# The second batch's q by bf16 split and crossbar transposes, and an earlier load of w_tok's last rows, in a fused attention and mixer kernel

## The chip, the cores and the metric

The kernel runs on one core of one Trainium2 chip. The metric is the device time of one execution in microseconds (us), lower is better. Each run carries its mean granted TensorE clock (1.0 is full speed) and a state: a run over 1.5% above the fastest of its kernel is called slow. Engines are called PE (TensorE), PEld (its weight loads), DVE (VectorE), ACT (ScalarE), POOL (GpSimd) and SP (SyncE, which issues nearly all DMAs here). In the profile, L549 is line 549 of the kernel.

## The reference, cut to what matters

```python
kv  = einsum('bhsd,bhse->bhde', k, v)          # batch 8, heads 8, seq 576, head_dim 64
out = einsum('bhsd,bhde->bhse', q, kv)
x   = out / sqrt(mean(out*out, -1) + 1e-6) * g_norm     # then heads are put side by side: d_model 512
a1  = alpha1 * x + beta1
tok = einsum('ts,bsd->btd', w_tok, a1)          # token mixing, 576 x 576
u   = x + lam * tok
a2  = alpha2 * u + beta2
ch  = maximum(a2 @ w_ch1, 0) @ w_ch2            # channel MLP, 512 -> 2048 -> 512
return u + lam * ch                             # all float32
```

## The kernel before

The eight batches run in a software pipeline: while PE works on the channel MLP of batch b, the attention and token mixing of batch b+1 and the k-by-v products of batch b+2 are slipped in between. A scheduler inside the kernel's own code decides, when the kernel is built, in which order each engine runs its instructions. It goes by costs written into the code (`P.op(engine, cost_us, ...)`). On the chip every engine then runs its list in that order. `at=` gives an operation a fixed rank, `slack` lets it be placed later. A wrong cost doesn't break anything, but it can leave the order a poor one.

Tile names met below: kf, vf and qf hold k, v and q as loaded; qs and qst the bf16 halves of q, qt and qtt the same transposed (qst and qtt for the tail rows); kvd the bf16 form of kv; sq and small the squares and sums of the normalisation, xm the rows of x and later of u, rt the bf16 input of the token mixing, wst and wt w_tok as loaded and transposed; a2b and a2t the MLP's input, ht its hidden values; stg the three staging buffers of the weights; ps is PSUM.

q must be transposed before the products q times kv. The first two batches (`R32 = 2`) do that on PE in fp32. From the third batch on, q is split into a high and a low bf16 half (ACT casts, DVE or POOL subtracts), and six DMA transposes through the crossbar, issued by SP, do the transposing:

```python
R32 = 2
...
def split_q(b):                       # five pieces: ACT makes hi, DVE or POOL makes lo = q - hi
    for x in range(5):
        ...
        P.op("ACT", act_us(n), lambda e, ...: copy(e, hi, src), r=kin, w=[("qs", x, 0)])
        P.op(dve_pool(n), 0, lambda e, ...: e.tensor_tensor(out=lo, in0=src, in1=hi, op=ALU.subtract), ...)

def qt_dma(b):                        # six transposes: four into qt, two for the tail into qtt
    for a in range(3):
        for y in range(2):
            ...
            P.op("SP", 1.3, lambda e, o=o, i_=i_: e.dma_start_transpose(o, i_), ...,
                 w=[("qt", a, y)], dma_us=0.8 if a < 2 else 0.3, slack=SLACK)
```

The loads leave SP in a fixed order. w0 to w3 are the 1 MB slices of W_ch1, w4 to w7 those of W_ch2, Bk, Bv and Bq the second batch's k, v and q, t0 to t2 rows of w_tok:

```python
order = ["k0", "v0", "q0", "k1", "t0", "v1", "q1", "t1",
         "w0", "g", "w1", "w2", "Bk", "Bv", "w3", "Bq", "lam", "a2", "t2", "w4",
         "w5", "w6", "w7"]
```

Each slice of W_ch2 is multiplied by lam on its way into bf16, on DVE or POOL, whichever the scheduler picks.

```python
for hh in range(4):
    P.op(dve_pool(512), 0, lambda e, hh=hh: e.tensor_tensor(              # L1270
        out=w2[:, 4 * n + hh, :], in0=stg[:, i % 3, hh], in1=lam_bc[:], op=ALU.mult), ...)
```

Of the kernel before, what the change touches and what calls it, by code (L numbers as in the profile page):

```python
# [403 lines left out]
def bass_transnormer_attn__then__resmlp_affine_kernel(  # L404
# [15 lines left out]
    with ExitStack() as stack:  # L420
        P = Prog(nc, stack)
# [27 lines left out]
        qtt = sb("qtt", [128, NH, 128], BF16)  # L449
# [47 lines left out]
        ALL = (slice(0, 8),)  # L497
        R32 = 2
        SLACK = 5.0
# [20 lines left out]
        def split_q(b):  # L520

            for x in range(5):
                if x < 4:
                    src = qf[:, x, 0:8].rearrange("p (k r) d -> p r k d", r=2)
                    hi, lo = (qs[:, x, :, i, :].rearrange("p (r k) d -> p r k d", r=2)
                              for i in range(2))
                else:
                    src = qf[:, :, 8, :]
                    hi, lo = (qst[:, :, i, :] for i in range(2))
                n = 512 if x < 4 else 256  # L530
                kin = [("qf", x // 2)] if x < 4 else [("qf", 0), ("qf", 1)]
                P.op("ACT", act_us(n), lambda e, hi=hi, src=src: copy(e, hi, src),
                     r=kin, w=[("qs", x, 0)])
                P.op(dve_pool(n), 0, lambda e, hi=hi, lo=lo, src=src: e.tensor_tensor(  # L534
                    out=lo, in0=src, in1=hi, op=ALU.subtract), r=kin + [("qs", x, 0)],
                    w=[("qs", x, 1)], port=True)

        def qt_dma(b):
            lo = 64 * (b % 2)
            for a in range(3):  # L540
                for y in range(2):
# [4 lines left out]
                    else:  # L546
# [4 lines left out]
                            for i in range(2)],  # L551
                         w=[("qt", a, y)], dma_us=0.8 if a < 2 else 0.3, slack=SLACK)

# [109 lines left out]
        def qkv_groups(b):  # L663

            def group(cs, hs):
# [20 lines left out]
                def f32(e):  # L686
                    if nc_ > 1:
                        for h in range(nh):
                            w = qtr[:, h0 + h, 2 * cs[0]:2 * cs[0] + 2, :].rearrange(
                                "p k s -> p (k s)")  # L690
                            for x in range(1 if nh < 8 else 2):
                                y = slice(0, 128) if nh < 8 else slice(64 * x, 64 * x + 64)
                                o = (t.flat().rearrange("p (c h d) -> p c h d", c=2, d=64)[
                                    :, :, h, :] if nh < 8 else t.cols(64 * (nh * x + h), 64))
                                mm = e.matmul(o, w, kvr[:, h0 + h, y], start=True, stop=True)  # L695
                    else:
                        for h in range(h0, hs.stop):
                            p = 64 * (h // 4)
                            mm = e.matmul(t.flat()[:, 64 * (h - h0):64 * (h - h0) + 64],
                                          qtrt[:, h % 4, :], kvr[:, h, p:p + 64],  # L700
                                          start=True, stop=True)
                    return mm
                if b < R32:
                    P.op("PE", 0.058 * m, f32, cold=True,
                         r=["qtp", "kvz"] + [("qtr", a, cs[0] if nc_ > 1 else 2) for a in aa] + [
# [42 lines left out]
                else:  # L748
# [14 lines left out]
                    out=x3, in0=x3, in1=gb, op=ALU.mult), r=xk + ["g"], w=xk, pri=-50, port=True)  # L763
            for hs in (HALVES if b == 0 else ALL):
                for cs in ((0, 2), (1, 3), (4,)):
                    yield lambda cs=cs, hs=hs: group(cs, hs)
# [313 lines left out]
        def params_late():  # L1080
            for key in ("e1r", "lamr", "gr", "er", "ebh", "ebl", ("pc", 0), ("pc", 1)):
                for n in range(4):
# [4 lines left out]
        order = ["k0", "v0", "q0", "k1", "t0", "v1", "q1", "t1",  # L1087
                 "w0", "g", "w1", "w2", "Bk", "Bv", "w3", "Bq", "lam", "a2", "t2", "w4",
                 "w5", "w6", "w7"]
# [7 lines left out]
        for x in range(2):  # L1097
            for u in (2 * x, 2 * x + 1):
# [3 lines left out]
        P.op("SP", 0.6, lambda e: e.dma_start(wst4[:], moe_w_tok[8:576:9, :]),  # L1102
             w=[("wst", 4)], dma_us=0.9, at=sp["t2"])
        for n, dst, src in (("lam", lam_bc, moe_lam), ("a2", a2_bc[:], moe_alpha2),
# [119 lines left out]
        def run(gens):  # L1224
            for gen in gens:
                for f in gen:
                    f()
# [59 lines left out]
        u0 = P.lastw[("a2t", 0)] + P.lastw[("a2t", 2)]  # L1287
        run([kv_groups(1), qt_groups(1)])
        for i in range(4, 8):
# [16 lines left out]
        for b in range(NB):  # L1306
# [5 lines left out]
            merge(ch1, list(qkv_groups(b + 1)), 0, len(ch1) * 5 // 8)  # L1312
            if b == 0:
                last = [o for a in range(2) for m in range(3) for o in P.readers[("qtr", a, m)]]
                for key in ([("qt", a, y) for a in range(3) for y in range(2)] +
                            [("qs", x, i) for x in range(5) for i in range(2)]):
                    P.readers.setdefault(key, []).extend(last)
            if more:
# [5 lines left out]
            if more:  # L1324
                if b == 0:
                    P.op("POOL", 0.9, lambda e: e.memset(qtt[:], 0.0),
                         w=[("qt", 2, y) for y in range(2)])
                split_q(b + 2)
                qt_dma(b + 2)
# [43 lines left out]
```

## Time and profile before

| | before |
|---|---|
| median of 3 runs (range) | 365.87 us (364.91 to 366.12) |
| span of the profiled run, clock | 364.2 us, 0.993 |
| PE busy | 357.3 us, 98% |
| longest PE wait on a DMA | 1.1 us, for w_tok's last rows |
| first MLP matmul of the second batch (L938) | 82.65 us |

SP's row says when a DMA is issued and how long the issue holds SP. Its columns are start, time, engine queue, line, operation, tiles, count. First the second half of the load phase, then, from the steady part of the kernel, the third batch's six transposes.

```profile
31.76 15.34 SPq L1265 DMA_DIRECT2D stg<-in_moe_w_ch_dram  x4
47.15 0.50 SPq L506 DMA_DIRECT2D kf<-in_k_dram  x1
...
79.67 7.24 SPq L549 DMA_TRANSPOSE qt<-qs  x4
86.95 3.19 SPq L549 DMA_TRANSPOSE qtt<-qst  x2
```

All four slices of W_ch2 are issued by 47.1. The third batch's transposes hold SP for 7.24 + 3.19 = 10.4 us.

### The profile page before, as it was taken

The page shows a single profiled execution, that of the slowest core. Times are in us where ns is not written, and L with a number is a line of the kernel's source. Part 1 is how long each engine was busy: PE and PEld are TensorE (multiplying, and loading weights), DVE is VectorE, ACT ScalarE, POOL GpSimd, SP SyncE. Part 2 cuts the span into 40 slices and gives each one's busy share as a digit, 9 for nine tenths or more (in the row PEclk, how much of TensorE's full clock was granted, in tenths as well). Part 3 has the DMA queues.
Part 4 walks back from the last instruction along what each step waited for, and adds up shares of the span by engine and source line. Part 5 has one row for each costly group of instructions (what it writes and reads, how often), then busy time and mean ns, then how long its engine had stood idle before and what let it go on. Part 6 is the DMA issues. An engine that isn't in the chain of part 4 may idle for free.

```text
span 364.2 us, 8018 instructions
## 1 busy us (share of the span) xinstructions
PE 357.3 (98%) x3594; PEld 215.2 (59%) x3354; DVE 211.4 (58%) x310; ACT 143.7 (39%) x252; POOL 116.2 (32%) x93
## 2 busy tenths in 40 slices
PE   8999899999999999999999999999999999999995
PEld 6888685466754554457654554457754554457644
DVE  3557699872686189823885189724884288620021
ACT  2675057127750158107730157007730156007500
POOL 4377185910064005700281015800751005300000
PEclk9999899999999999999999999999999999999999
DMA  7999996028865677667816684586836510340023
GB/s 286 355 384 363 323 350 250 0 49 113 237 249 117 115 202 283 104 125 170 314 32 127 117 277 174 108 123 142 337 66 124 117 29 2 72 96 21 2 58 86
DMA packets 67558, 59.17 MB, mean 162 GB/s; under 512 B 45552, under 2 KB 45828, under 8 KB 67524
## 3 DMA queue, kind: packets, MB, share of 16 engines
q1 hardware_dynamic: 67472, 58.66, 58.4%
q8 instruction: 27, 0.44, 0.5%
q14 instruction: 7, 0.06, 0.0%
q10 hardware_dynamic: 52, 0.01, 0.0%
HBM read 38.60 MB, written 9.44 MB: 132 GB/s over the span
## 4 chain that ended last, share of the span: by engine, by line
PE 91%; DMA 5%; SPq 2%; ACT 1%; issue 0%; DVE 0%
PE ps L988 34%; PE ps L938 19%; PE ps L923 13%; PE ps L787 8%; PE ps L602 5%; DMA wst<-in_moe_w_tok_dram 3%; DMA vf<-in_v_dram 3%; PE ps L397 2%; PE ps L682 2%; PE ps L1146 2%; PE ps L800 1%; PE ps L695 1%; PE ps L570 1%; SPq L506 1%; PE ps L1189 0%; SPq L1106 0%
## 5 line engine op out<-in xcount | busy, mean ns | idle before, releaser
L988 PE MATMUL ps<-w,ht 128*128 128x512 bf16 (+1 forms) x592 | 129.0, 373 | 0.0
L988 PEld LDWEIGHTS ps<-w,ht 128*128 128x128 bf16 x592 | 56.8, 98 | 64.1 <-issue 1.6
L912 ACT ACTIVATE ht<-ps,bias 128x640 bf16<-128x640 f32 (+2 forms) x98 | 72.5, 742 | 46.4 <-PE ps L938 38.7
L938 PE MATMUL ps<-a2t,w 128*128 128x320 bf16 x512 | 71.9, 299 | 0.0
L762 POOL TENSOR_TENSOR xm<-xm,g_bc 128x1024 f32<-128x1024 f32 (+1 forms) x16 | 33.4, 2085 | 114.9 <-DVE rt L759 112.4
L938 PEld LDWEIGHTS ps<-a2t,w 128*128 128x128 bf16 x512 | 49.5, 98 | 20.3 <-DVE xm L755 0.3
L923 PE MATMUL ps<-a2t,w 128*128 128x512 bf16 x240 | 54.6, 379 | 0.0
L999 DVE TENSOR_TENSOR xm<-ps,xm 128x512 f32<-128x512 f32 (+1 forms) x33 | 22.1, 673 | 53.4 <-PE ps L988 53.4
L633 ACT ACTIVATE kvd<-ps 64x256 bf16<-64x256 f32 x24 | 9.1, 378 | 99.8 <-PE ps L602 99.6
L733 DVE TENSOR_REDUCE small<-sq 128x16 f32<-128x1024 f32 (+3 forms) x27 | 24.8, 928 | 22.9 <-ACT sq L731 22.7
L923 PEld LDWEIGHTS ps<-a2t,w 128*128 128x128 bf16 x240 | 22.7, 98 | 25.1
L787 PE MATMUL ps<-rt,wt 128*128 128x512 bf16 x140 | 31.4, 379 | 0.0
L913 DVE TENSOR_SCALAR ht<-ps,bias 128x512 bf16<-128x512 f32 (+2 forms) x34 | 24.8, 738 | 10.3 <-PE ps L923 4.7
L534 POOL TENSOR_TENSOR qs<-qf,qs 128x512 bf16<-128x512 f32 x14 | 18.5, 1319 | 25.8 <-ACT qs L493 24.8
L731 ACT ACTIVATE sq<-ps 128x1024 f32<-128x1024 f32 (+3 forms) x27 | 21.3, 799 | 12.9 <-PE ps L397 8.2
L771 DVE TENSOR_TENSOR xm<-ps,xm 128x512 f32<-128x512 f32 x28 | 19.1, 688 | 8.9 <-PE ps L787 8.6
L787 PEld LDWEIGHTS ps<-rt,wt 128*128 128x128 bf16 x140 | 13.7, 98 | 16.5
L999 DVE TENSOR_TENSOR xtl<-ps,xtl 128x512 f32<-128x512 f32 x4 | 2.8, 692 | 35.5 <-PE ps L988 35.5
L602 PEld LDWEIGHTS ps<-vf,kf 64*64 64x64 f32 x1152 | 18.9, 140 | 3.5 <-issue 2.5
L602 PE MATMUL ps<-vf,kf 64*64 64x64 f32 x1152 | 20.1, 227 | 0.4 <-DMA vf<-in_v_dram 0.2
L755 DVE TENSOR_TENSOR xm<-ps,small 128x1024 f32<-128x1024 f32 (+1 forms) x18 | 19.7, 1100 | 0.2
L759 POOL TENSOR_TENSOR rt<-xm,e_bc 128x512 bf16<-128x512 f32 (+1 forms) x6 | 9.8, 1635 | 28.4 <-DVE xm L755 27.4
(105 smaller groups left out, 349.5 us busy)
## 6 DMA issues: line engine op xcount, KB each, us to landing
stg<-in_moe_w_ch_dram SPq DMA_DIRECT2D x8, 1024.0 KB, 12.5
kf<-in_k_dram SPq DMA_DIRECT2D x7, 1152.0 KB, 6.6
vf<-in_v_dram SPq DMA_DIRECT2D x7, 1152.0 KB, 8.7
qf<-in_q_dram SPq DMA_DIRECT2D x7, 1152.0 KB, 10.2
out_dram<-xm SPq DMA_DIRECT2D x62, 128.0 KB, 2.4
kf<-in_k_dram SPq DMA_DIRECT2D x2, 576.0 KB, 5.7
vf<-in_v_dram SPq DMA_DIRECT2D x2, 576.0 KB, 9.4
qf<-in_q_dram SPq DMA_DIRECT2D x2, 576.0 KB, 8.3
```

The costliest lines, as they stand in the source:

```text
L602: m = e.matmul(t.ap(slice(64 * i, 64 * i + 64))[:, y, 64 * x_:64 * x_ + 64], kf[rows, x, c], vf[rows, x, c], start=(c == 0), stop=(c == 8) ...
L731: P.op("ACT", act_us(64 * m), lambda e: e.activation(both(sqv), raw(), ACT.Square), r=[t], w=[("sq", sqs)])
L733: P.op("DVE", dve_us(64 * m), lambda e: e.tensor_reduce(out=smv, in_=sqv, axis=AX.X, op=ALU.add), r=[("sq", sqs)], w=[("sm", sms)], pri=-20)
L755: P.op("DVE", dve_us(64 * m), lambda e: e.tensor_tensor(out=x3, in0=raw(), in1=inv(), op=ALU.mult), r=[t, ("sm", sms)], w=xk, pri=-200)
L762: P.op(dve_pool(64 * m) if b < 2 else "POOL", pool_us(64 * m), lambda e: e.tensor_tensor(out=x3, in0=x3, in1=gb, op=ALU.mult), r=xk + ["g" ...
L787: m = e.matmul(t.flat(), wt[:, sc if sc < 4 else 4 + b % 2, 128 * c:128 * c + 128], rt[:, rs(b, sc), :], start=(sc == 0), stop=(sc == 4))
L912: return e.activation(dst, src(), ACT.Relu, bias=bi)
L913: return e.tensor_scalar(out=dst, in0=src(), scalar1=bi, scalar2=0.0, op0=ALU.add, op1=ALU.max)
L923: m = e.matmul(t.flat(), w1[:, dj, 128 * fj:128 * fj + 128], a2t[:, dj, 0:512], start=(dj == 0), stop=(dj == 3))
L938: m = e.matmul(t.ap()[:, i, 0:320], w1[:, dj, 128 * fj:128 * fj + 128], a2t[:, dj, 320 * i:320 * i + 320], start=(dj == 0), stop=(dj == 3))
L988: m = e.matmul(t.flat()[:, 0:m_], ht[:, fj, 128 * c:128 * c + 128], w2[:, fj, lo:hi], start=(fj == 0), stop=(fj == 15))
L999: P.op("DVE", dve_us(m_), lambda e: e.tensor_tensor(out=x, in0=t.flat()[:, 0:m_], in1=x, op=ALU.add), r=[t] + keys, w=keys)
```

## The change

The intent: take the second batch's fp32 transposes and products off PE, which is the bound, by treating that batch like the later ones. To make room, the splits get a rank ahead of W_ch1's last casts, the six transposes get a place ("x") in the load order ahead of W_ch2's last three slices, and w_tok's last rows (t2) go ahead of W_ch1's fourth slice. The scheduler's cost of the remaining fp32 products was corrected too.

```diff
-        R32 = 2
+        R32 = 1
...
                 P.op("ACT", act_us(n), lambda e, hi=hi, src=src: copy(e, hi, src),
-                     r=kin, w=[("qs", x, 0)])
+                     r=kin, w=[("qs", x, 0)], at=-958.5 if b == 1 else None)
... (the same rank for the five subtractions)
-                         w=[("qt", a, y)], dma_us=0.8 if a < 2 else 0.3, slack=SLACK)
+                         w=[("qt", a, y)], dma_us=0.8 if a < 2 else 0.3,
+                         at=sp["x"] + 0.01 * (2 * a + y) if b == 1 else None,
+                         slack=SLACK if b > 1 else 1.0)
...
-                    P.op("PE", 0.058 * m, f32, cold=True,
+                    P.op("PE", 0.1 + (0.06 if nc_ > 1 else 0.12) * m, f32, cold=True,
...
-                 "w0", "g", "w1", "w2", "Bk", "Bv", "w3", "Bq", "lam", "a2", "t2", "w4",
+                 "w0", "g", "w1", "Bq", "w2", "t2", "w3", "lam", "w4", "Bk", "Bv", "x", "a2",
                  "w5", "w6", "w7"]
...
-             w=[("wst", 4)], dma_us=0.9, at=sp["t2"])
+             w=[("wst", 4)], slack=4.0, dma_us=0.9, at=sp["t2"])
...
-        run([kv_groups(1), qt_groups(1)])
+        run([kv_groups(1)])
+        P.op("POOL", 0.9, lambda e: e.memset(qtt[:], 0.0), w=[("qt", 2, y) for y in range(2)])
+        split_q(1)
+        qt_dma(1)
         for i in range(4, 8):
             load_w(i)
... (cut: the fp32 path's code for two batches, and moved bookkeeping)
```

## The prediction

> **What bounds the kernel now.** I read the page first, its engine totals, then its clock row. PE (TensorE) counts as busy for 98% of the span, and the chain that ended last is 91% PE.
>
> ```profile
> PE 357.3 (98%) x3594; PEld 215.2 (59%) x3354; DVE 211.4 (58%) x310; ACT 143.7 (39%) x252; POOL 116.2 (32%) x93
> ...
> PE 91%; DMA 5%; SPq 2%; ACT 1%; issue 0%; DVE 0%
> ```
>
> The reader is to see that no other engine comes near PE, so PE work taken away should come off the end, as long as nothing new stops PE. Next I read the chain of waits in order of time (start, length, what) around the part that the change rewrites, the second batch's attention, at 31 to 55 us.
>
> ```profile
> 31.09 10.16 DMA wst<-in_moe_w_tok_dram
> 41.25 0.14 issue
> 41.38 1.24 PE ps L1146 x16
> ...
> 42.82 3.13 PE ps L602 x138
> ...
> 46.31 1.02 PE ps L570 x8
> 47.34 0.22 PE ps L563 x2
> 47.56 0.86 PE ps L923 x4
> 48.42 0.87 PE ps L570 x8
> 49.29 0.22 PE ps L563 x2
> 49.51 0.86 PE ps L923 x4
> 50.38 3.49 PE ps L695 x32
> 53.87 0.88 PE ps L923 x4
> 54.75 0.81 PE ps L699 x8
> 55.56 4.33 PE ps L923 x20
> ...
> 79.58 2.26 PE ps L602 x144
> ```
>
> L570 and L563 are the fp32 transposes of q, L695 and L699 the fp32 products of q with kv, L602 the k-by-v products, L923 and L988 the channel MLP that fills the time between. The one DMA in this stretch that PE waits for is the transfer of w_tok's last rows (wst): issued at 31.09, landed 10.2 us later. Then I cut PE's row into half microseconds (length, PE busy and instructions, granted clock, DMA share, GB/s).
>
> ```profile
> 40.50:41.00 0.50, 0.00 (x0) 1.00 0.94 283
> 41.00:41.50 0.50, 0.12 (x2) 1.00 1.05 389
> ...
> 42.50:43.00 0.50, 0.50 (x24) 0.50 1.01 373
> ...
> 44.50:45.00 0.50, 0.50 (x30) 0.52 1.05 389
> 45.00:45.50 0.50, 0.50 (x44) 1.00 1.05 389
> ```
>
> This view shows what the busy share hides. PE stands still from 40.24 to 41.38 (1.14 us), and just behind that the granted clock is 0.5 from about 41.5 to 45.0. That is the only half-clock stretch of the run; the 4 us slices from 80 us on are all at 1.00 until the last matmuls.
>
> **What the Trainium skill says.** (1) "TensorE: Matmul & The Clock Gate", Part 1: the array's clock drops to half when a monitoring window of about 3.4 us sees too little PE activity, and comes back after a busy one. The trace agrees on the length (3.5 us at 0.5) but not on the cause as put there, idleness of a whole window: here 1.14 us of idle, beside 0.94 us of two-column bias matmuls, were enough. (2) The same page, LDWEIGHTS: load time follows the weight's columns, not its contraction rows. So cutting the first batch's tail products from 128 to 64 rows (one part of the diff) should give nothing; the trace has no 64-row twin to show it. (3) "DMA: Bandwidth & Descriptors", Rules for kernel authors: a DMA transpose must not run beside one from another queue, but next to ordinary DMAs it needs nothing. All transposes here leave from SP, so none has to be held for that; the trace's batches 3 to 8 already run them so.
>
> **The change, part by part.**
>
> *Removed from PE.* Both transpose groups of the second batch: 46.31 to 47.56 is 1.25 us, 48.42 to 49.51 is 1.09. The products: 50.38 to 53.87 is 3.49, 54.75 to 55.56 is 0.81. Sum 6.64 us, all on the chain.
>
> *Added to PE.* The bf16 form of the same products, as the third batch has them: in its chain they take 92.59 to 94.46 (1.87 us, 64 matmuls) and 96.63 to 97.10 (0.47 us, 16), together 2.34 us. Net 6.64 - 2.34 = **4.30 us off PE**. The k-by-v products stay fp32.
>
> *The w_tok rows ahead of W_ch1's fourth slice.* Before, their issue stood behind that slice's, which waited until 28.32 for a staging buffer, and behind q, lam and alpha2. Now they stand behind slice 3 only, which waits for no buffer; q of the second batch, ahead of it, can go once the first batch's q is transposed (L563 runs at 16.1). By 30 us the DMA of before had moved some 10 MB at about 344 GB/s; in the new order everything up to these rows is 9.1 MB, so about 27 us (an estimate from that rate). PE gets there at 40. So the **1.14 us** gap goes.
>
> *The half clock behind it.* In it the L602 group makes some 61 matmuls per us (30 or 31 per half microsecond), against 98 in the group at 79.58. From 42.7 to 45.0 that is 141 matmuls in 2.3 us in place of 1.4: 0.9 us. The transposes of the w_tok rows before it (1.3 us) would at the same ratio lose another 0.4 to 0.5. If the gap was what tipped the window, **1.3 us** more go. Sum of all gains: 4.30 + 1.14 + 1.3 = 6.7 us.
>
> *Added beside PE.* Five ACT casts for the high halves (the third batch: 4 of 0.615 and 1 of 0.40: 2.9 us), five subtractions (0.68 on DVE or 1.23 on POOL for the large ones: 3.2 to 5.8 us), a 0.95 us memset on POOL that only moves, and six crossbar transposes. From 33 to 46.3 us ACT is busy 2.9 of 13.3 us, POOL 3.7, DVE 9.4: there is room. Evacuations of fp32 q and kv (10 groups on ACT and DVE) become the bf16 pairs for kv. The six transposes take SP from 79.67 to 90.14 in the third batch, 10.5 us. If the splits are done at about 36, their issue ends near 47, the last landing near 49 (2.4 to 4.5 us from issue to landing).
>
> *Moved.* k and v of the second batch now go after W_ch2's first slice. With a DMA at 350 to 390 GB/s from 28 us on (two slices of 1.05 MB, k and v of 1.18 MB each, some 0.3 MB of lam) they land near 43 to 44, by estimate. Before, their products ran at 42.7. W_ch2's slices 2 to 4 now leave behind the transposes, so from about 47, and land near 51 to 58; their first use is about four groups into the L988 run, now near 57.
>
> *What holds the end.* PE work between 39.3 and the second batch's MLP (82.4 before) becomes 43.1 - 6.7 = 36.4 us, so that it would start at 75.7. The dependent path is: transposes landed and kv split at about 49 to 50, new products to about 53, normalisation (55.4 to 63.8 before, but other PE work filled that; DVE's last rt is done at 62.7, so 7.3 us), token mixing 61 to 66.5, then the alpha2 products and transposes (69.7 to 77.9 before: 8 us), so ready near 75. The two paths end within a microsecond of each other. I therefore take **0.8 us** off the gain for stalls: 6.7 - 0.8 = 5.9, and 365.87 - 5.9 = 360.0.
>
> **Rivals.** (a) *The crossbar route comes late.* SP works in a fixed order, splits, then 10.5 us of transposes, then the rest of W_ch2; queued data is 20 MB up to 60 us with the DMA over 0.84 busy nearly all along. If q lands late or the splits slip by 3 us, the new products, token mixing or W_ch2's slice stop PE for 2 to 4 us, and a stop could bring the half clock again. Against: about 20 us of independent MLP work lies there as a filler. This would make 362 to 364. (b) *The splits push W_ch1's casts.* They rank ahead of the last eight casts and of the evacuations of PSUM; late slices 3 and 4 would stop PE near 40 us, 1 to 2 us and perhaps the half clock: 361.5 to 363. For: slice 4 lands only at about 33 to 34. Against: ACT runs nothing from 37 to 42.7 in the profile of before. (c) *More than counted.* The corrected costs of fp32 products may give the scheduler a better start (PE runs warm-up fillers at 26 and 31 us), and the early w_tok rows may fill such holes: up to 1.9 us for their transposes and sums, 358 to 359. Against: their stated slack of 4 us should hold them until after the start. (d) *The clock stays low.* If small matmuls, not the gap, tip the window, 1.3 us remain: 361.3.
>
> **Range and chances.** The clean sum gives 359.2, so 2% (under 358.55) needs all terms and some of (c): 0.15. Rivals (a), (b) and (d) have about one chance in three together and lead to 361.3 to 364. Slower by 2% would need 13 us of new stalls on top of the gain: 0.01. I say 360.0, with 357.8 to 362.9 at 8 in 10.
>
> **What would show it.** Right: no fp32 group of L695's 64-column form any more; 40 more pairs of bf16 products taking 2.3 us; no PE wait on wst; clock 1.00 from 39 to 46; L602's second group at about 2.3 us; the second batch's MLP starting at 75 to 77. Wrong: a PE wait of over 1 us between 36 and 76 us on the transposes, on stg casts or on kf and vf; a new half-clock stretch; or a start (first MLP matmul at 32.2 us) that has moved by more than 1 us either way.

## The result and the profile after

The changed kernel took **375.64 us** (median of 4 runs, 373.78 to 376.42), the kernel before 365.51 in its 4 runs. The ratio is 1.027, with a 95% interval of 1.023 to 1.031: slower. Ratios here and below are the mean time of one kernel's fast runs over that of the other's of the same rounds, so not quite the ratio of the medians. An unedited repeat later (r_after) gave 1.029.

The page of the kernel after, its span, PE's total and the chain that ended last by engine and by line:

```profile
span 374.6 us, 7987 instructions
PE 355.0 (95%) x3578; PEld 211.1 (56%) x3331; DVE 210.4 (56%) x315; ACT 146.2 (39%) x257; POOL 113.3 (30%) x91
PE 71%; DVE 10%; SPq 7%; POOL 4%; DMA 4%; issue 2%; ACT 1%; POOLq 0%
PE ps L988 27%; PE ps L938 14%; PE ps L923 11%; PE ps L787 8%; SPq L549 6%; PE ps L604 4%; DVE rt L759 3%; DMA stg<-in_moe_w_ch_dram 3%; PE ps L1335 2%; PE ps L684 2%; PE ps L397 2%; DMA qf<-in_q_dram 2%; DVE a2b L773 1%; POOL qs L534 1%; POOL w L494 1%
```

By these profiles PE is busy 2.3 us less than before, and the span is 10.4 us longer. So PE idle time grew from 6.9 to 19.6 us. The chain, 91% PE before, is now 71% PE. A new line stands in it: L549, the issue of the six transposes by SP, 6% of the span. The waits of PE (line, what it waited for, total us, times, longest) name the stops:

```profile
PE ps L988 <- DVE w L1270: 4.6, 1, 4.6
PE ps L787 <- DVE rt L759: 3.0, 3, 1.8
PE ps L604 <- DMA vf<-in_v_dram: 2.1, 1, 2.1
PE ps L1335 <- DVE eps L1115: 1.1, 1, 1.1
PE ps L938 <- ACT ht L912: 0.9, 1, 0.9
PE ps L988 <- DVE xm L755: 0.8, 1, 0.8
```

The wait for w_tok's rows is gone, as intended (the 1.1 us at L1335 is the start of the kernel and stood there before). Of the 3.0 us for rt, 2.5 lie in later batches. SP's row and the chain say where the new stops come from. First SP's row:

```profile
31.83 0.51 SPq L506 DMA_DIRECT2D vf<-in_v_dram  x1
36.67 13.05 SPq L549 DMA_TRANSPOSE qt<-qs  x4
49.77 3.25 SPq L549 DMA_TRANSPOSE qtt<-qst  x2
53.06 0.58 SPq L1106 DMA_DIRECT2D a_bc<-in_moe_alpha_dram  x1
53.70 1.54 SPq L1265 DMA_DIRECT2D stg<-in_moe_w_ch_dram  x3
```

The six transposes hold SP for 13.05 + 3.25 = **16.3 us**, against 10.4 in the third batch of the kernel before. The tail pair takes the same (3.25 and 3.19); it is the first four that grew, 7.24 to 13.05. W_ch2's slices 2 to 4 can't be issued until 53.70. The chain of waits in order of time (start, length, what) shows the rest:

```profile
42.02 4.10 SPq L549
...
46.16 1.31 SPq L549
...
53.70 0.43 SPq L1265
...
54.17 10.37 DMA stg<-in_moe_w_ch_dram
...
64.56 0.69 DVE w L1270
65.25 2.26 DVE small L733 x2
...
72.04 1.93 DVE rt L759
...
74.74 0.61 PE ps L787 x2
```

The first transpose took 5.30 us (36.67 to 41.97), the second 4.10, the third 1.31. The slow ones end at 46.12, close to when the v load, issued before them, lands (PE waits for it until 46.43). The chain hangs the end of the first one on POOL's memset of qtt, which ends at 41.89. That is not what held it: in e7 below the memset ends at 41.03 and the first transpose at 42.75, and in e12 two transposes are through before the memset starts (40.9). Three slices and the next batch's q, k and v then leave within 10 us of each other and share the DMA. DVE's row (in brackets: idle time and what ended it) shows how this spreads:

```profile
61.85 2.49 DVE L1270 TENSOR_TENSOR w<-stg,xtl 128x512 bf16<-128x512 f32 x4 [8.84 <-DMA stg<-in_moe_w_ch_dram]
64.56 0.69 DVE L1270 TENSOR_TENSOR w<-stg,xtl 128x512 bf16<-128x512 f32 x1 [0.21 <-DMA stg<-in_moe_w_ch_dram]
65.17 2.34 DVE L733 TENSOR_REDUCE small<-sq 128x16 f32<-128x1024 f32 x2
```

The new bf16 products were done at 56.2, but in DVE's fixed order the multiplication of W_ch2's slices stands ahead of the reductions that normalise them (L733). What the reductions read are ACT's squares:

```profile
55.02 1.96 ACT L731 ACTIVATE sq<-ps 128x1024 f32<-128x1024 f32 x2 [0.25 <-PE ps L397]
```

So DVE stood still for 8.84 us (53.0 to 61.8), the last 5 of them with both inputs there, and came to the reductions at 65.17, 8.2 us after the second was ready. The dependent path (reductions, rt, token mixing) came late. Two windows (length, busy time of PE, PEld, DVE, ACT, POOL with instructions, granted clock, DMA share, GB/s):

```profile
14.00:17.00 3.00, 3.00 (x75) 2.82 (x69) 2.07 (x7) 0.57 (x2) 1.26 (x1) 0.50 1.02 379
...
60.00:64.50 4.50, 0.10 (x1) 0.10 (x2) 2.49 (x4) 0.00 (x0) 0.00 (x0) 1.00 1.04 392
64.50:68.50 4.00, 4.00 (x12) 1.43 (x11) 3.88 (x6) 1.29 (x4) 3.74 (x3) 0.57 1.06 392
```

PE is idle for 4.4 of 4.5 us from 60, and the clock is halved behind that. A second half-clock stretch lies in the head of the kernel, at 14 to 17 us. It wasn't there in the profiled run of before, and the first MLP matmul starts at 33.9 instead of 32.2. The second batch's MLP starts at 89.5 us, 6.9 later than before; from there to the end it is 285.1 us, against 281.6 before. So a third of the loss, 3.5 us, lies behind the second batch's start. There PE waits 0.9 us for ht and 2.5 us for rt, in r_after too; before, it waits for nothing. The longest of these waits (1.8 us, at 119 us, third batch) hangs by the chain on ACT, where casts of the next q, which landed at 111.0, stand ahead of a step of the third batch's normalisation.

### The profile page after: what moved, and what is told of

It is laid out like the page before. It is cut to its first block, busy times and chain, and to the rows that moved or that the text cites. A ratio compares the mean times of both kernels' runs of the same rounds, so it can differ in the third digit from the quotient of the medians.

```text
span 374.6 us, 7987 instructions
## 1 busy us (share of the span) xinstructions
PE 355.0 (95%) x3578; PEld 211.1 (56%) x3331; DVE 210.4 (56%) x315; ACT 146.2 (39%) x257; POOL 113.3 (30%) x91
## 4 chain that ended last, share of the span: by engine, by line
PE 71%; DVE 10%; SPq 7%; POOL 4%; DMA 4%; issue 2%; ACT 1%; POOLq 0%
PE ps L988 27%; PE ps L938 14%; PE ps L923 11%; PE ps L787 8%; SPq L549 6%; PE ps L604 4%; DVE rt L759 3%; DMA stg<-in_moe_w_ch_dram 3%; PE ps L1335 2%; PE ps L684 2%; PE ps L397 2%; DMA qf<-in_q_dram 2%; DVE a2b L773 1%; POOL qs L534 1%; POOL w L494 1%
## 5 line engine op out<-in xcount | busy, mean ns | idle before, releaser
L988 PE MATMUL ps<-w,ht 128*128 128x512 bf16 (+1 forms) x571 | 128.1, 377 | 7.2 <-DVE w L1270 4.6
L988 PEld LDWEIGHTS ps<-w,ht 128*128 128x128 bf16 x592 | 57.1, 98 | 71.4 <-DVE w L1270 5.1
L912 ACT ACTIVATE ht<-ps,bias 128x640 bf16<-128x640 f32 (+2 forms) x99 | 73.5, 745 | 51.1 <-PE ps L938 39.6
L762 POOL TENSOR_TENSOR xm<-xm,g_bc 128x1024 f32<-128x1024 f32 (+1 forms) x16 | 34.9, 2181 | 109.6 <-DVE rt L759 108.2
L923 PE MATMUL ps<-a2t,w 128*128 128x512 bf16 x231 | 52.6, 379 | 0.6 <-issue 0.2
L635 ACT ACTIVATE kvd<-ps 64x256 bf16<-64x256 f32 x28 | 10.6, 378 | 109.0 <-PE ps L604 108.8
L733 DVE TENSOR_REDUCE small<-sq 128x16 f32<-128x1024 f32 (+3 forms) x27 | 24.5, 928 | 30.2 <-ACT sq L731 30.0
L913 DVE TENSOR_SCALAR ht<-ps,bias 128x512 bf16<-128x512 f32 (+2 forms) x33 | 23.4, 721 | 14.4 <-PE ps L923 9.7
L534 POOL TENSOR_TENSOR qs<-qf,qs 128x512 bf16<-128x512 f32 x13 | 15.4, 1182 | 50.4 <-ACT qs L493 49.6
L773 POOL TENSOR_TENSOR a2b<-xm,a_bc 128x512 bf16<-128x512 f32 x11 | 16.7, 1517 | 12.9 <-DVE xm L771 12.7
## 6 DMA issues: line engine op xcount, KB each, us to landing
qf<-in_q_dram SPq DMA_DIRECT2D x7, 1152.0 KB, 10.4
```

The source lines that it names most:

```text
L733: P.op("DVE", dve_us(64 * m), lambda e: e.tensor_reduce(out=smv, in_=sqv, axis=AX.X, op=ALU.add), r=[("sq", sqs)], w=[("sm", sms)], pri=-20)
L762: P.op(dve_pool(64 * m) if b < 2 else "POOL", pool_us(64 * m), lambda e: e.tensor_tensor(out=x3, in0=x3, in1=gb, op=ALU.mult), r=xk + ["g" ...
L912: return e.activation(dst, src(), ACT.Relu, bias=bi)
L913: return e.tensor_scalar(out=dst, in0=src(), scalar1=bi, scalar2=0.0, op0=ALU.add, op1=ALU.max)
L923: m = e.matmul(t.flat(), w1[:, dj, 128 * fj:128 * fj + 128], a2t[:, dj, 0:512], start=(dj == 0), stop=(dj == 3))
L988: m = e.matmul(t.flat()[:, 0:m_], ht[:, fj, 128 * c:128 * c + 128], w2[:, fj, lo:hi], start=(fj == 0), stop=(fj == 15))
```

## The experiments

The explanation, **theory A**: beside a full DMA the six transposes hold SP far longer than the 10.4 us assumed, so W_ch2 comes late and blocks DVE. **Rival B**: it is the new load order as such (k and v later). **Rival C**: not SP's queue but the transposes themselves are the problem; they get through slowly beside the loads, whoever issues them. Further rivals were the splits' rank ahead of W_ch1's casts and the changed cost figure. Every kernel gave a correct result. The runs of one group went to one chip and share the runs of the kernel before.

| run | median us (before, same group) | ratio, 95% interval | clock, profiled run |
|---|---|---|---|
| e1_tok_early | 369.63 (365.75) | 1.009, 1.004 to 1.014 | 1.000 |
| e2_order_only | 364.82 (365.75) | 0.997, 0.995 to 0.999 | 1.000 |
| e3_x_behind_w6 | 373.35 (365.75) | 1.022, 1.018 to 1.025 | 0.982 |
| e4_true_issue | 372.63 (365.75) | 1.018, 1.016 to 1.020 | 0.986 |
| e5_kv_early | 371.57 (366.34) | 1.012, 1.005 to 1.019 | 0.991 |
| e6_pe_transposes | 367.83 (366.34) | 1.003, 0.996 to 1.010 | 0.995 |
| e7_old_costs | 373.25 (366.34) | 1.017, 1.009 to 1.024 | 0.991 |
| e8_splits_last | 371.71 (366.34) | 1.013, 1.002 to 1.024 | 0.989 |
| r_after | 376.41 (366.15) | 1.029, 1.023 to 1.035 | 0.982 |
| e9_pe_old_order | 366.47 (366.15) | 1.001, 1.000 to 1.003 | 1.000 |
| e10_act_issue | 380.20 (366.15) | 1.035, 1.029 to 1.040 | 0.973 (slow) |
| e11_pe_kv_early | 365.12 (366.15) | 0.997, 0.996 to 0.999 | 0.993 |
| e12_x_first | 379.68, one run (366.00) | not timed | 0.982 |
| e13_x_best | 373.01 (366.00) | 1.021, 1.013 to 1.028 | 0.995 |
| e14_pe_pool | 365.61 (366.00) | 0.998, 0.993 to 1.002 | 0.995 |
| e15_fp32_pool | 363.60 (366.00) | 0.994, 0.989 to 1.000 | 0.999 |

The medians of e8 and e10 take in one slow run each; the ratios leave it out. In the second and fourth group the runs of the kernel before spread over 5 us, so medians across groups are compared to 1 or 2 us at best.

Where the time lies, from the profiled run of each (us):

| run | first MLP matmul | second batch's MLP starts | from there to the end |
|---|---|---|---|
| before | 32.2 | 82.7 | 281.6 |
| the changed kernel; r_after | 33.9; 33.8 | 89.5; 89.5 | 285.1; 285.6 |
| e3 | 33.9 | 92.7 | 281.1 |
| e4 | 33.9 | 89.2 | 282.7 |
| e5 | 32.5 | 88.9 | 281.2 |
| e6 | 33.0 | 85.0 | 281.1 |
| e7 | 33.6 | 89.1 | 282.5 |
| e8 | 32.4 | 86.7 | 281.1 |

The last column matters for what follows: the 3.5 us that the changed kernel loses there are gone in e3, e5 and e8, which keep the crossbar transposes. So they come with the order of the later batches and not with the transposes' duration as such, which is longest in e3.

### First group: the parts alone, and the transposes' place

**e1_tok_early**: the kernel before, with w_tok's last rows ahead of W_ch1's fourth slice, nothing else.

```diff
-  ... "w2", "Bk", "Bv", "w3", "Bq", "lam", "a2", "t2", "w4",
+  ... "w2", "Bk", "Bv", "t2", "w3", "Bq", "lam", "a2", "w4",
-             w=[("wst", 4)], dma_us=0.9, at=sp["t2"])
+             w=[("wst", 4)], slack=4.0, dma_us=0.9, at=sp["t2"])
```

> The kernel before with one move only: w_tok's last rows ahead of W_ch1's fourth slice (and their stated slack of 4 us). If the gap at 40.2 us and the half clock behind it are both due to the late rows, 2.0 to 2.6 us come off: about 363.3. If the half clock comes from the small matmuls and not from the gap, only about 1.1 us: about 364.7. If another wait takes its place: no change.

Measured: 369.63, slower than before by 0.9%. The wait for the rows went, but PE's groups between 42 and 47 us (busy time, mean ns of one, then idle before and its cause) show a stop of 2.0 us in the middle of the k-by-v products, for which the trace shows no releaser:

```profile
L602 PE MATMUL ps<-vf,kf 64*64 64x64 f32 x144 | 2.6, 221 | 2.0 <-issue 2.0
```

Three of the four runs also had a lower clock (0.986 to 0.991). What follows: the 1.14 us of the gap was not there for the taking. Another stop took its place.

**e2_order_only**: the kernel before in fp32, with the changed kernel's whole load order (t2's slack included).

```diff
-  "w0", "g", "w1", "w2", "Bk", "Bv", "w3", "Bq", "lam", "a2", "t2", "w4",
+  "w0", "g", "w1", "Bq", "w2", "t2", "w3", "lam", "w4", "Bk", "Bv", "x", "a2",
```

> The kernel before (q of the second batch by fp32) with the whole load order of the changed one, without any crossbar transpose for the second batch. Theory A (the transposes on SP hold up W_ch2's second slice): no long wait on W_ch2, at most the 2.1 us wait on k and v; 362.5 to 366. Rival B (the moved loads themselves cost the time, through k and v behind W_ch2's first slice and through the DMA's hole at 27 to 31 us): over 369.

Measured: 364.82, 0.3% faster than before, with a clock of 1.0 in every run and a 1.7 us stop for v in the place of the old gap. Rival B falls: the load order alone isn't where 10 us went.

**e3_x_behind_w6**: the changed kernel, with the transposes behind W_ch2's slices 2 and 3.

```diff
-  ... "w4", "Bk", "Bv", "x", "a2", "w5", "w6", "w7"]
+  ... "w4", "Bk", "Bv", "w5", "w6", "x", "a2", "w7"]
```

> The changed kernel with the six transposes of the second batch issued behind W_ch2's second and third slices in place of ahead of them. Theory A: the second slice is issued near 34 to 38 us and lands before 50; PE's 4.6 us wait and the half clock at 65 to 68 us go, the second batch's chain moves up; 361 to 367. Rival C (the crossbar transposes take the DMA's throughput wherever they stand): the slices or the products stay late, over 371.

Measured: 373.35, only 1% or less better than the changed kernel. The slices were now early (issued at 33.46 to 40.53), and no wait on L1270 was left. But the transposes, started at 40.58 beside those slices, took longer still. Their line in the trace (min, median, max ns; first and last start):

```profile
L549 SPq DMA_TRANSPOSE qt<-qs x4: 1322/2942/8297, 40.6 to 54.9; - x4
```

One of them took 8.3 us. PE now waited for qt and qtt (0.8 and 1.9 us), for v (2.9) and for the late normalisation (4.2). The loss changed its place and stayed. That speaks against the form of theory A in which only the slices behind the transposes suffer.

**e4_true_issue**: the changed kernel, with the scheduler told about the measured cost of the transposes.

```diff
-                    P.op("SP", 1.3, lambda e, o=o, i_=i_: e.dma_start_transpose(o, i_),
+                    P.op("SP", 1.3 if b > 1 else 2.7, lambda e, ...
-                         w=[("qt", a, y)], dma_us=0.8 if a < 2 else 0.3,
+                         w=[("qt", a, y)], dma_us=(0.8 if a < 2 else 0.3) if b > 1 else 1.8,
```

> The changed kernel; only the scheduler's cost of these six transposes is put nearer to what was measured (2.7 us of SP each in place of 1.3, 1.8 us in the DMA). Load order as changed. Theory A: W_ch2's second slice is still issued near 53 us, but the static order of DVE no longer puts its products ahead of the second batch's reductions, so that part of the loss goes: 368 to 373. If the blocked DVE is not part of the loss: as the changed kernel, 375.

Measured: 372.63. The wait on L1270 is gone, since the scheduler no longer puts that work in front of the reductions; PE waits 5.5 us for rt and 1.6 for xm instead. The right cost wins 3 to 4 us (by the medians, 375.64 and 376.41 against 372.63, across groups), but not by removing that stop: from 30 us to the second batch's MLP PE waits 9.4 us in all, against 9.2 and 7.1 in the two profiles of the changed kernel, and that MLP starts only 0.4 us earlier. What is won lies behind it (282.7 us against 285.1), where the waits for rt are gone. The lateness itself remains.

### Second group: the other parts of the change

**e5_kv_early**: the changed kernel with k and v ahead of t2 and W_ch1's fourth slice.

```diff
-  "w0", "g", "w1", "Bq", "w2", "t2", "w3", "lam", "w4", "Bk", "Bv", "x", "a2",
+  "w0", "g", "w1", "Bq", "w2", "Bk", "Bv", "t2", "w3", "lam", "w4", "x", "a2",
```

> The changed kernel with k and v of the second batch ahead of w_tok's last rows (so issued near 18 to 20 us instead of 31), the six transposes still behind W_ch2's first slice. Theory A2 (a transpose takes 4 to 5 us of SP only while megabytes of loads lie ahead of it in the DMA; alone it takes 1.3 to 2): the first two transposes take about 2 us each, W_ch2's second slice is issued near 47 to 49 in place of 53.7, the wait on v goes; 363 to 369. Rival A1 (a transpose costs SP 3 us at this stage whatever lies ahead): W_ch2's slice near 53 again, 371 to 374.

Measured: 371.57. The transposes took 14.0 us in all (3.15, 3.25, 2.27, 2.02, 1.88, 1.25). The stop before the k-by-v products was still 1.8 us, though the trace no longer shows PE waiting for v there. W_ch2's slices 2 to 4 left at 50.92. The issue lies between what theory A2 and rival A1 expected, the time in A1's range. Better than the changed kernel, still 1.2% slower than before.

**e6_pe_transposes**: the changed kernel with everything kept (splits, bf16 products, load order), but the 36 bf16 blocks of 128 by 128 are transposed on PE and copied out of PSUM by ACT and DVE. No crossbar transpose is left in the second batch.

```diff
+        def qt_pe(b):          # nine groups of four transposes into one PSUM bank, one copy each
+            ... m = e.transpose(t..., qs[:, x, c0 + j].rearrange("p i d -> p (i d)"), identb[:])
+            ... copy(e, qt[:, :, x, c0:c0 + 4, :], ...)
-        qt_dma(1)
+        qt_pe(1)
```

> The changed kernel with the bf16 splits and the bf16 products of the second batch kept, but the nine transposes made on PE in bf16 (36 of 128 by 128, about 1.9 us of PE) in place of the six on the crossbar. Theory A (the crossbar route, SP's time in front of W_ch2's slices, is what costs; the bf16 products are worth what was counted): no wait on W_ch2, 361 to 365. Rival D (the splits and their rank, or the bf16 pairs for kv, cost the time too): over 368.

Measured: 367.83, on a par with before. This is the main finding: with the crossbar route taken out and PE given more work, the kernel gets some 8 us faster than the changed one (by the medians, across groups; 375.64 and 376.41 against 367.83). Not all of it is the crossbar's doing in the load phase. By the profiled runs 0.9 us lie before the first MLP matmul (this run has no half-clock stretch in the head, those of the changed kernel have one), 3.6 between it and the second batch's MLP, and 4.0 behind. And theory A's 361 to 365 was missed: even without the crossbar the products' saving doesn't show. PE's largest waits here:

```profile
PE ps L642 <- DMA vf<-in_v_dram: 4.1, 3, 2.7
PE ps L961 <- ACT ht L950: 1.6, 1, 1.6
```

No wait on rt, xm or L1270 is left (L642 is the k-by-v group; this kernel's lines are shifted by 38). What remains is the late v.

**e7_old_costs**: the changed kernel with the old cost figure for the first batch's fp32 products.

```diff
-                    P.op("PE", 0.1 + (0.06 if nc_ > 1 else 0.12) * m, f32, cold=True,
+                    P.op("PE", 0.058 * m, f32, cold=True,
```

> The changed kernel with the scheduler's cost of the first batch's fp32 products put back to 0.058 us each group and head; no instruction differs but their order. If the later start of the first MLP matmul (33.9 us against 32.2) comes from that figure, it is back at 32 to 32.5 us and the half clock at 13.9 to 17 us is gone; 1 to 2 us faster than the changed kernel (373.5 to 374.5). If it comes from the place of the monitor's window or from other parts of the change: 33.9 again.

Measured: 373.25, with the same wait on L1270 (5.3 us) and a half-clock stretch in the head (13.1 to 16.5 us). The cost figure isn't the cause of either. The kernel is still 2.4 to 3.2 us faster than the changed one by the medians (across groups), 2.6 of it behind the second batch's start by the profiles; so the figure may have cost something through the order there, which wasn't tested again.

**e8_splits_last**: the changed kernel with the splits ranked behind W_ch1's casts.

```diff
-                     r=kin, w=[("qs", x, 0)], at=-958.5 if b == 1 else None)
+                     r=kin, w=[("qs", x, 0)], at=-956.5 if b == 1 else None)   # both split ops
```

> The changed kernel with the rank of the splits undone: behind W_ch1's last casts in place of ahead of slice 3's. Theory A: the casts end earlier and the splits a few us later, so the transposes start later than 36.7 us, W_ch2's second slice later than 53.7: 375 to 379. Rival B (the rank costs time through W_ch1's casts): faster than the changed kernel by 1 us or more.

Measured: 371.71 over five runs, one of them slow at 377.35; ratio 1.013. The transposes started 2.5 us later (39.17) but held SP for 8.6 + 3.4 = 12.0 us instead of 16.3, and W_ch2's slices left at 51.88, earlier than in the changed kernel. Started later, when more of the loads had landed, the transposes finished earlier. That is against theory A's forecast here (375 to 379) and as rival B's: the splits' rank was itself harmful. How it did harm is only in part known. This variant has no half clock in the head either, and of the 6.8 us between its profiled run (its fastest) and that of the changed kernel 1.5 lie before the first MLP matmul, 1.3 between it and the second batch's MLP, and 4.0 behind.

### Third group: who issues, and bf16 without the crossbar

**r_after**: the changed kernel, unedited, once more.

> The changed kernel once more, unedited, beside the others of this call, because the kernel before spread from 364.3 to 369.6 us in the last call. As measured first: 374 to 376. Whether the half clock at 13.9 to 17 us (seen in the changed kernel and three variants, not in three others) is there again tells if it belongs to the order of instructions or comes and goes.

Measured: 376.41, ratio 1.029. The transposes held SP for 13.02 + 3.20 us, as in the first look. The stops fell differently: 3.5 us for xm, 2.8 for v (1.9 of it for the second batch's), 2.5 for rt and 1.0 for L1270. The delay is stable; which PE instruction meets it is not.

**e9_pe_old_order**: bf16 products and PE transposes in the load order of before, with the late rank of the splits.

```diff
+  (e6's qt_pe, R32 = 1, splits at -956.5)
   "w0", "g", "w1", "w2", "Bk", "Bv", "w3", "Bq", "lam", "a2", "t2", "w4", "w5", "w6", "w7", "x"]
```

> The load order of the kernel before, bf16 splits behind all of W_ch1's casts, bf16 transposes on PE, bf16 products: nothing of the change left but the bf16 arithmetic. If the saving on PE is worth what was counted (6.6 us of fp32 against 1.9 + 2.3 us of bf16), 362.5 to 364. If splits and evacuations on ACT, DVE and POOL at this stage cost as much as they save: 365 to 368.

Measured: 366.47, ratio 1.001. PE's work for the second batch's q is smaller than before, and none of it reaches the end: 1.8 us go in a wait for ht, 1.4 in a stop at the k-by-v products with no releaser in the trace.

**e10_act_issue**: the changed kernel, with the six transposes issued from ACT's queue, so that SP is free for W_ch2's slices.

```diff
-                    P.op("SP", 1.3, lambda e, o=o, i_=i_: e.dma_start_transpose(o, i_),
+                    P.op("SP" if b > 1 else "ACT", 1.3 if b > 1 else 1.7, lambda e, ...
-                         at=sp["x"] + 0.01 * (2 * a + y) if b == 1 else None,
+                         at=None,
```

> The changed kernel with the six transposes of the second batch issued from ACT's queue in place of SP's, placed by the scheduler among ACT's other work at 1.7 us each. SP then goes on to W_ch2's slices at once (second slice near 37 us). Theory A (SP's fixed order is what holds W_ch2 back): no wait on W_ch2's products, 363 to 369. Rival C (the crossbar traffic among megabytes of loads is late or slow by whichever queue): the second batch's products late, 371 or more.

Measured: 380.20, the worst of the timed runs (fast runs 376.37 to 380.40). The profiled run was slow, so only the order of magnitude of its times is used. SP issued W_ch2's slices from 34.63 on. ACT's row, then PE's longest wait:

```profile
36.60 16.34 ACTq L549 DMA_TRANSPOSE qt<-qs  x3
53.00 5.02 ACTq L549 DMA_TRANSPOSE qt<-qs  x1
```

```profile
PE ps L1189 <- ACT wt L493: 10.2, 1, 10.2
```

The first three transposes held ACT for 16.3 us, and PE waited 10.2 us for a cast that stood behind them on ACT. Here too the transposes took their time from the engine that issued them. Between theory A in its queue-only form and rival C, rival C stands.

**e11_pe_kv_early**: e6 with the load order of e5 and the late rank of the splits.

```diff
-  "w0", "g", "w1", "Bq", "w2", "t2", "w3", "lam", "w4", "Bk", "Bv", "x", "a2",
+  "w0", "g", "w1", "Bq", "w2", "Bk", "Bv", "t2", "w3", "lam", "w4", "x", "a2",
-  at=-958.5
+  at=-956.5
```

> The variant with bf16 transposes on PE, with k and v of the second batch loaded ahead of w_tok's last rows and the splits behind W_ch1's casts. If its 2.7 us wait on v and the half clock behind it were what kept it from gaining, 362.5 to 365. If another stall takes that place (as the 1.8 us inside the k-by-v group did where k and v came early): 366 to 368.

Measured: 365.12, 0.3% faster than before, in a very narrow range (365.00 to 365.25). The stop at 40 to 46 us is gone. A 2.0 us wait for ht on DVE came instead. This run does have the half-clock stretch in the head (0.50 from 14 to 17 us) and still has the lowest median of the bf16 variants (e14's ratio is the same).

### Fourth group: the transposes alone, the best crossbar version, the best version

**e12_x_first**: the changed kernel with the transposes ahead of W_ch2's first slice and of k and v, so that little else is in the DMA. A bad order on purpose; one look only, its state unknown.

```diff
-  ... "w3", "lam", "w4", "Bk", "Bv", "x", "a2",
+  ... "w3", "lam", "x", "w4", "Bk", "Bv", "a2",
```

> The changed kernel with the six transposes ahead of W_ch2's first slice, k and v in SP's order, so with nothing but W_ch1's last slice in the DMA in front of them. If a transpose is slow only while loads stand in front of it, the first two take 1.3 to 2.7 us of SP each in place of 5.3 and 4.1, the six together 10 to 12 us in place of 16.3. If they are as slow, the DMA's load is not what makes them so. The time itself gets worse, since k, v and W_ch2 now start near 48 us: 380 to 390.

Measured: SP's row of this kernel, then the window over the six transposes (columns as before):

```profile
36.78 7.18 SPq L549 DMA_TRANSPOSE qt<-qs  x4
44.01 3.19 SPq L549 DMA_TRANSPOSE qtt<-qst  x2
```

```profile
36.80:47.20 10.40, 10.32 (x92) 5.93 (x91) 7.29 (x14) 1.74 (x5) 4.72 (x5) 1.00 0.76 110
```

7.18 + 3.19 = **10.4 us**, the duration of the third batch, at the same place of the kernel (36.78 against 36.67) where the changed kernel needs 16.3. Only what else is in the DMA differs: 110 GB/s here, against 400 from 36.6 to 41.9 in the changed kernel. This settles the transposes' time. The kernel took 379.68 us, because k, v and W_ch2 were held up by those 10.4 us and only then loaded; PE was busy for 2.95 of the 9.8 us from 47.2 to 57.0.

**e13_x_best**: everything learned put together for the crossbar: k and v early, splits late, slice 2 of W_ch2 ahead of the transposes, a truer cost.

```diff
-  "w0", "g", "w1", "Bq", "w2", "t2", "w3", "lam", "w4", "Bk", "Bv", "x", "a2", "w5", "w6", "w7"]
+  "w0", "g", "w1", "Bq", "w2", "Bk", "Bv", "t2", "w3", "lam", "w4", "w5", "x", "a2", "w6", "w7"]
-  P.op("SP", 1.3, ...), dma_us=0.8 if a < 2 else 0.3
+  P.op("SP", 1.3 if b > 1 else 2.2, ...), dma_us=(0.8 if a < 2 else 0.3) if b > 1 else 1.6
   (and splits at -956.5)
```

> The best arrangement of the crossbar route that the study suggests: k and v early, the splits behind W_ch1's casts, W_ch2's first two slices ahead of the transposes, and a cost of 2.2 us a transpose for the scheduler. If the route itself can pay here, 362 to 365; if its 10 to 16 us of SP and its late landing cannot be hidden at this stage, 366 to 370.

Measured: 373.01. The transposes held SP from 37.80 to 52.32 (11.83 + 2.65 us), slices 3 and 4 left at 53.00, and PE waited 5.2 us for an rt on POOL. That is slower than either forecast: the pieces that helped singly don't add up. In no place tried did the crossbar route pay in this load phase.

**e14_pe_pool** is e11 with the multiplications of W_ch2's slices 2 to 4 on POOL alone, so that they can't block DVE. **e15_fp32_pool** is the kernel before (fp32 q) with e5's load order and that same rule.

```diff
-                    P.op(dve_pool(512), 0, lambda e, hh=hh: e.tensor_tensor(
+                    P.op(dve_pool(512) if n < 1 else "POOL", pool_us(512), lambda e, hh=hh: e.tensor_tensor(
```

> The variant with bf16 transposes on PE and early k and v, with the products of W_ch2's slices 2 to 4 kept off DVE (POOL only), because in its trace DVE stood in such products at 51 to 56 us and PE then waited 2.0 us for DVE. If that is so, 363 to 364.5; if POOL is then late with the slices, 365 or more.

> The same load order and the same POOL rule with the second batch's q by fp32 as before: tells how much of the last variant's gain is the bf16 path. If the bf16 path is worth its 2.4 us of PE, this one is 1 to 2.5 us slower than that one; if it is worth nothing, equal to it within 0.5 us.

Measured: 365.61 and 363.60. PE's largest wait in e14, then in e15:

```profile
PE ps L825 <- POOL rt L797: 2.4, 1, 2.4
```

```profile
PE ps L1336 <- DVE eps L1115: 1.1, 1, 1.1
PE ps L988 <- issue: 1.0, 6, 0.2
```

In e15 nothing stops PE for more than 0.3 us between the start and the last instructions, its clock is 0.999, and the second batch's MLP starts at 80.4 us. It has the lowest median found, 0.6% below before (two of its six runs took 365.4 and 366.8), and it uses none of the bf16 path. Neither forecast for it held. e14 pays for its rt wait and for a half-clock stretch behind it (clock 0.74 from 62 to 66 us). How much of e15's gain comes from the load order and how much from the POOL rule wasn't separated: e2's order without either the early k and v or the rule gave 0.3%, and the rule by itself brought e14 nothing over e11.

## Why the prediction was wrong

**The saving on PE was right, but it never reached the end.** The bf16 products took 53.88 to 56.19, 2.3 us, against 2.34 foretold, and the fp32 transposes and products (6.64 us) are gone. The busy total can't confirm the 4.30 us: it shows 2.3 us less in this profile and 1.0 us more in r_after's, which has 33 more matmul records of the same kernel. The prediction's point (2), on weight loads, can be read now: the first batch's tail loads took 187 ns with 64 rows, against 192 with 128 before, as it said.

**The step that failed** is the sentence "If the splits are done at about 36, their issue ends near 47, the last landing near 49", together with "land near 51 to 58" for W_ch2. It took 10.5 us for the six transposes from the third batch, where the DMA carried 131 GB/s, and put them into a phase that the same text calls over 0.84 busy. Three terms were off:
- The splits: the first pair was ready at 36.65 as assumed, but all low halves went to POOL behind its casts; the last was done at 40.1 and the memset for the tail at 41.9. No transpose is seen waiting for these, as the issue of the first one lasted until 41.97 anyway.
- The issue: 16.3 us instead of 10.4, so it ended at 53.0 rather than 47. e12 shows that the load makes the difference: 10.4 us at the same place without it.
- W_ch2: issued together at 53.70 and sharing the DMA with the next batch's loads, slice 2 came 8.2 us later, at 61.85, not 4 us after its issue. Put together, that is 11 us later than the early end of the predicted range. Token mixing, put at 61, began at 74.74.

**Rival (a) was the right mechanism, sized too small.** It said 362 to 364, with stops of 2 to 4 us. Its argument against itself failed: the MLP work that was to serve as filler (L988) needs W_ch2, which stood in the same queue behind the transposes, and PE stopped there for 4.6 us. The stop was followed by a half-clock stretch (64.9 to 68.4), as (a) had mentioned. The fixed order of DVE, with L1270 ahead of the normalisation, gave the stop its shape but isn't shown to have lengthened it: in e4, without that order, token mixing began at 67.77, yet PE waited no less and the second batch's MLP came only 0.4 us earlier. And 3.5 us more were lost behind that point, in waits for ht and rt that no part of the prediction covers.

**Rival (b), splits pushing casts**, was true in an unexpected form. PE hardly stopped for W_ch1. But e8, which only ranks the splits behind the casts, wins 4 to 5 us by the medians (across groups, and with the head's half clock gone as well): the transposes then start 2.5 us later, beside fewer loads, and end 1.8 us earlier. Most of that gain lies in later batches, as said there.

**The gap and the half clock behind it (2.4 us)** were wrongly counted as gains. The wait for w_tok's rows did go, and the clock was at 1.00 from 40 to 45 us in the changed kernel. But a wait for v of 2.1 us stood in its place. e1, which does that part alone, is slower than before; e2 gains 0.3%. Only with k and v early (e11, e13, e15) was the stop gone, and e5 still had 1.8 us of it. The estimate "they land near 43 to 44" failed too: v landed at 46.4, 14.6 us after its issue, sharing the DMA with the transposes. (The figures given with it, some 4.8 MB from 28 us at 350 to 390 GB/s, come to 40 to 42.)

**The start** moved by 1.7 us (33.9 against 32.2), the prediction's own sign of error. The half-clock stretch at about 14 to 17 us goes with it; it is in both profiled runs of the changed kernel, in e3, e4, e7 and e11, and not in e5, e6, e8 and e13. It follows no single edit, so its cause stays open. It can explain at most 1 to 2 us of the 10, and it is part of the 8 us between e6 and the changed kernel.

**What the sum would have needed.** With no crossbar at all (e6, e9, e11, e14) the bf16 arithmetic lands between 0.997 and 1.003 of before. In one group, the fp32 version e15 is 2.0 us below its bf16 twin e14 by the medians, 1.3 by the means, with ranges that overlap: no gain from bf16, and not clearly a loss. So "PE busy 98%" was read too simply: the second batch lies in the load phase, where PE's order waits on data, and work taken off PE there turned into waiting.

**What stays open**: the stop of 1.4 to 2.0 us at the k-by-v products around 43 us, for which the traces of e1, e5 and e9 show no releaser; the half clock in the head; the 3.5 us behind the second batch's start, which come and go with the order; and the division of e15's gain.

## What to carry to other kernels

The issue time of a crossbar transpose must be taken from a stretch with the same DMA load as the one that it is put into: six of them held SP for 16.3 us here with about 400 GB/s of loads ahead of them and for 10.4 without, and all that SP had still to issue waited with them. Before moving work off the busiest engine in a load phase, ask which transfer that engine will wait for next: less work there was worth nothing here, where the data set the pace. And when an experiment removes a stop, look at when the next stage starts, not only at the total: e4 removed one, gained 3 to 4 us, and gained it elsewhere.

## What the Trainium skill lacked or had wrong

- "DMA: Bandwidth & Descriptors", Rules for kernel authors, says that a transpose next to ordinary DMAs needs nothing. It says so of correct results, and there the runs agree. Of time it has nothing: four transposes held SP for 13.05 us beside about 400 GB/s of loads falling off to 150, and for 7.18 us at 110 GB/s; single ones took 5.3 and 8.3 us instead of 1.4 to 2.0. From ACT's queue beside W_ch2's slices three of them took 16.3 us. The page gives no figure for how long an issue holds the issuing engine under load.
- "VectorE: DVE Perf Modes", The three transpose paths, gives 1309 ns for a 128 by 128 bf16 tile by the crossbar and 390 ns on TensorE. No run moves such a tile alone by the crossbar; of the second batch's transposes in the changed kernel, one of 64 rows by 2048 columns took 6.7 us from issue to landing, one of 64 by 512 took 2.4. On PE the 36 tiles took 219 ns each in the profile, overlapping. The page doesn't say that the first figure depends on what else the DMA carries.
- "TensorE: Matmul & The Clock Gate", Part 1, puts the half clock, in its table of states, down to an idle window of about 3.4 us. The stretches here have about that length, but in the kernel before 1.14 us of idle preceded one, and ahead of the one at 14 to 17 us in the changed kernel PE counts as busy in the profile for 3.49 of 3.50 us (10.4 to 13.9). What tips it isn't settled here.
- No page has the stop of 1.4 to 2.0 us at the k-by-v products (43 to 46 us) for which the trace names no releaser.
